# Splitting a scan of decays around an inverse, and spreading the loads of two chunks

## The chip, the cores and the metric

The kernel runs on one core of a Trainium2 chip. What is compared is the device time of one launch in microseconds (us), from runs of the same program on the same inputs. The core has five instruction streams that matter here. TensorE (PE in the profile) multiplies matrices, VectorE (DVE), ScalarE (ACT) and GpSimd (POOL) work elementwise, and SyncE (SP) gives out nearly all transfers (DMA). Each works through its own list in order, and waits for the others by semaphores.

## The reference

There are two parts, one behind the other. The first is a recurrence over 768 time steps, for 4 batches and 8 heads of width 40. Each head has a 40 x 40 state:

```
for t in range(S):
    y[:, :, t] = einsum('bhd,bhde->bhe', rt, state)
    Sa = einsum('bhde,bhe->bhd', state, at)
    state_decay = state * wt[:, :, None, :] - einsum('bhd,bhe->bhde', Sa, bt)
    state = state_decay + einsum('bhd,bhe->bhde', vt, kt)
```

The second part takes y as 3072 tokens of 320 numbers: `h = x @ w_in`, `g = h * cos(h)`, `out = g @ w_out`, with 2048 hidden numbers per token. The weights w_in and w_out arrive in 64-bit floating point, all other inputs in 32-bit.

## The kernel before, in words

**Chunks.** Time is cut into 24 chunks of 32 steps. The four batches lie on the four blocks of 32 partitions, so one tile holds one chunk of all batches and heads. Within a chunk the recurrence becomes matrix products with a triangular inverse per head and batch. From chunk to chunk only the state goes on, in the tile qz.

**Preparing a chunk.** `p1` has four parts for two chunks at a time: `p1_w` (decays), `p1_a` (a times the decays, aT), `p1_b` (b over the decays, turned: bT) and `p1_n` (their products, nps, copied to nt). `over_w` takes 1/w on VectorE (L395, rw) and b times that on POOL (L396, bn). `p2` prepares k, v and r of one chunk (vT, rT, kT, gram). `main(c)` is the chain of a chunk, in five steps t, q, x, s, z: the state turned (sT), qps, x0ps, sps, and dps with the new state (L754 on VectorE, L755 on POOL) and the outputs yt. `tokens` stores yt to DRAM (xd, L775) and its `back` loads it again as the tokens' tile xT (L785, L787). The second part multiplies xT.

**The decays.** For chunks 0 to 3 the running products of w are taken on the turned tile (L374). For chunks 4 and up they are taken beforehand, for four chunks at once, in the tile ws of 128 x 32 x 40. `ws_fetch(q)` loads it from w (L161, 640 KB). `ws_scan(q)` multiplies it in place in two halves: five instructions upward (L170) and four downward (L175), all on VectorE. `ws_store(q)` writes it to DRAM as wd (L180, 640 KB). `load(c, "w")` of a chunk from 4 on reads wd. `scanned(q)` is the scan, with the store two steps later and the next fetch twelve steps later. There is one tile ws, so a fetch needs the store before it to be done. In the part before the main loop `scanned(1)` comes right after chunks 0 to 3 are prepared, ahead of the inverse.

**The inverse.** `by_blocks(0)` holds its steps for chunks 0 to 3: a transpose of nt (L486, u), 15 pairs of instructions (L520, L525), and two transposes (L534, L502: the tile rt). `pair_first` and `pair_second` fill in the lower half with products on TensorE (below), and VectorE adds it (L567) before step s of that chunk may use rt.

**The weights.** They are rounded from 64-bit to 32-bit words in 20 units. Each unit is fetched by SP (L237, words), opened on VectorE (L245, L246), completed by `mantissa` (L255, with ScalarE at L258), and multiplied together (L261 on VectorE, L264 on POOL). Fetching a unit takes a buffer that an earlier one has to give back: unit 10 takes that of unit 7, unit 14 that of unit 11.

**What sets the order.** All is written out by hand. The order of the calls is the order in each engine's list. `step(work, of_inv, of_w)` makes a step, then counts down the works that wait in a list, then gives out some steps of the inverse and of the weights. `later(n, work)` puts a work into that list, to be given out after n more steps. Works that fall to the same step go in the order in which they were put in. Most of them are loads, and SP's list is in order: a DMA that waits for its data or its buffer holds up all behind it.

**Loads.** `load(c, names)` gives out four DMAs of 40 KB, one per batch, in pieces of 160 bytes (L152). Chunks 0 and 1, and 4 and up, take turns in two tiles for each of w, a and b (nat_w, nat_a, nat_b). Chunks 2 and 3 lie for the time being in parts of the weights' tiles (that of b in w_out_sb). Chunks 4 and 5 are loaded by a list at the end of the part before the main loop (L1028); chunks 6 and up by `p1` itself.

**The main loop.** For each chunk c a list `segs` names the steps of the chunk's chain, those of the next chunks' preparation, and places M for pieces of the second part. In chunks 1 and 2, the steps F and S are `pair_first` and `pair_second`. In chunk 3, `pw4`, `pa4`, `pb4` and `pn4` prepare chunks 4 and 5. `busy` and `kept_busy` are matmuls on a tile of zeros that keep TensorE at work.

Of the kernel before, what the change touches and what calls it, by code (L numbers as in the profile page):

```python
# [20 lines left out]
def kernel(  # L21
# [124 lines left out]
    def load(c, names, via=nc.sync, parts=range(B)):  # L146
        for n in names:
            for i in parts:
                at_c = src[n][i, :, c * C : (c + 1) * C, :]
                if n == "w" and c >= 4:  # L150
                    at_c = wd[c // 4][i, :, c % 4]
                via.dma_start(nat[n, c][blk[i], :, :D], at_c.rearrange("h t d -> t h d"))  # L152
# [6 lines left out]
    def ws_fetch(q, via=nc.sync):  # L159
        n = 4 * C * D  # L160
        via.dma_start(  # L161
            ws.rearrange("p t d -> p (t d)"),
            bass.AP(w.tensor, w.offset + q * n, [[S * D, B * H], [C * D, 4], [1, C * D]]),
        )

    def ws_scan(q):
        n = 1
        while n < C:
            to = ws[:, 2 * n - 1 :: 2 * n]
            nc.vector.tensor_tensor(to, to, ws[:, n - 1 :: 2 * n], ALU.mult)  # L170
            n *= 2
        n = C // 4
        while n:
            to = ws[:, 3 * n - 1 :: 2 * n]
            nc.vector.tensor_tensor(to, to, ws[:, 2 * n - 1 : C - 1 : 2 * n], ALU.mult)  # L175
            n //= 2

    def ws_store(q):
        wd[q] = dram.tile([B, H, 4, C, D], F32, tag="wd", name="wd")
        nc.sync.dma_start(wd[q].rearrange("b h c t d -> (b h c) (t d)"), ws.rearrange("p t d -> p (t d)"))  # L180
# [5 lines left out]
    load(1, "a", nc.scalar)  # L186
    for n, c in (("w", 2), ("w", 3), ("a", 2), ("a", 3), ("b", 2)):
        load(c, n)
    ws_fetch(1)
    load(3, "b")  # L190

# [149 lines left out]
    def later(steps, work):  # L343
        waiting.append([steps, work])

    def step(work, of_inv=0, of_w=0, small=False):


        before = list(waiting)
        work()  # L350
        G["small"] = small and G["kind"]
        for w in before:
            w[0] -= 1
            if w[0] == 0:
                waiting.remove(w)
                w[1]()
        for steps, n in ((inv_steps, of_inv), (w_steps, of_w)):
            for _ in range(min(n, len(steps))):
                steps.pop(0)()
# [186 lines left out]
    def pair_first(c, i, moe=True):  # L546
        ps = pair_space(c, moe, ps_h, "h")
        nt = G["noff"].rearrange("p c e j t -> p (c e j) t")
        half = pair_half(c, i)
        for n in range(H):  # L550
            for g in range(B):
                mm(
                    ps[blk[g], HB * n : HB * (n + 1)], nt[blk[g], H * i + n, :],
                    G["rn"][blk[g], H * i + n, :], n == 0,
                )
        nc.scalar.copy(half[:, :, :HB], ps[:, : H * HB].rearrange("p (n u) -> p n u", u=HB))
        if c + i == 3:
            nc.gpsimd.memset(padding(bn_b[6]), 0.0)
# [347 lines left out]
    def scanned(q):  # L906

        ws_scan(q)
        later(2, lambda: ws_store(q))
        if q + 1 < NCH // 4:  # L910
            later(12, lambda: ws_fetch(q + 1))
# [17 lines left out]
    with tc.manual_schedule():  # L929
# [63 lines left out]
        w_work[1][0]()  # L993
        for seg in (other[1], *first[2:], *other[2:]):
            step(seg)
        scanned(1)
        p2_in(0)
        p2_kn(0)
        inv_space()
# [17 lines left out]
        step(g1)  # L1017
        busy(3)
        N_PAD = {0: 0, 19: 60}
        step(lambda: pair_first(0, 0, False), 0, 2)  # L1020
        for m in range(3, 5):
            w_work[m][0]()
        step(lambda: pair_second(0, 0, False), 0, 2)
        step(s0, 0, 4)
        busy(6)
        step(z0, 0, 2)
        busy(4)
        for n, c, name in ((1, 4, "a"), (3, 4, "w"), (5, 5, "w"), (6, 5, "a"), (7, 5, "b"), (9, 4, "b")):  # L1028
            later(n, lambda c=c, name=name: load(c, name))

        done = 0
# [17 lines left out]
        for c in range(NCH):  # L1049
            t, q, x, s, z = main(c)  # L1050
            v, k, g = p2(c + 1) if c + 1 < NCH else [lambda: None] * 3
            q0 = c - c % 4 + 4
            fill, pn, pn4 = (1, 4), None, None
            if c == 0:
                segs = []
            elif c == 1:
                segs, fill = [t, F1, v, q, k, S1, x, g, s, z], (1, 4)
            elif c == 2:
                segs, fill = [t, F2, v, q, S2, k, M, x, M, F3, g, M, s, S3, M, z, M, M], (0, 2)
            elif c == 3:  # L1060
                pw4, pa4, pb4, pn4 = p1(4)
                pw, pa, pb, pn = p1(6)
                segs = [
                    t, pw4, M, q, pa4, M, x, lambda: scanned(2), M, s, pw, M, pb4, pa, M, pn4, M, z, M,
                    pb, v, pn, k, M, g,
                ]
                fill = (2, 3)
            elif c == 4:
                pw, pa, *p8 = p1(8)
                firsts = [lambda n=n: pair_first(4, n) for n in range(4)]  # L1070
                seconds = [lambda n=n: pair_second(4, n) for n in range(4)]
                F4, F5, F6, F7 = firsts
                S4, S5, S6, S7 = seconds
                segs = [
                    t, v, M, q, M, k, x, M, F4, M, S4, F5, M, s, F6, M, pw, F7, M, z, M, g, M, pa, S5, lambda: scanned(3),
                ]
                fill = (2, 0)
            elif c == 5:
                pw, pa = p1(10)[:2]
                pb, pn = p8  # L1080
                segs = [t, M, pb, q, M, pn, k, M, x, M, s, S6, M, z, M, S7, M, pw, v, M, g, pa, M]
            elif c % 4 == 0 and q0 < NCH:
                pb, pn = p1(q0)[2:]
                segs = [t, v, M, q, M, k, x, M, g, M, s, pb, M, z, M, pn, M, M]
                if q0 + 4 < NCH:
                    segs.insert(-1, lambda: scanned(c // 4 + 2))
            elif c % 4 == 1 and q0 < NCH:
                pw, pa = p1(q0 + 2)[:2]
                segs = [t, M, pw, q, M, x, k, M, s, v, M, z, M, pa, M, g, M, M]
            elif c % 4 == 2 and q0 < NCH:  # L1090
                pb, pn = p1(q0 + 2)[2:]
                segs = [t, M, pb, q, M, pn, v, M, x, M, s, k, M, g, M, z, M, M]
            elif c % 4 == 3 and q0 + 4 < NCH:
                pw, pa = p1(q0 + 4)[:2]
                segs = [t, M, pw, q, M, x, k, M, s, v, M, z, M, pa, M, g, M, M]
            else:
                segs = [t, v, M, q, M, x, k, M, g, M, s, M, M, z, M, M]
            n = len(segs)

            goal = 8 * (c + 1) - (18 if c < 19 else 20)  # L1100
            empty, places = 0, segs.count(M)
            if c > 3:
                empty = max(0, min(places - (goal - done), 2 if c < 8 else places))
                goal = max(goal, done + places - empty)
            place = 0
            if c == 19:
                shifted(N_PAD[c])
            for i, seg in enumerate(segs):
                kept_busy(FILL.get((c, i), 0))
                while seg is s and ("rt", c) not in G:  # L1110
                    if allowed(c):
                        piece(4, 0)
                    else:
                        inv_steps.pop(0)()
                while seg is pn4 and w_steps:
                    w_steps.pop(0)()
                if seg is not M:
                    G["kind"] = "q" if seg is q and c > 3 else "other"
                    step(seg, *((0, 0) if c < 3 and seg in (*firsts, *seconds) else fill), small=seg in (q, x, g, s, z, pn, pn4, *firsts, *seconds))
                    if seg not in (*firsts, *seconds) and (c < 2 or c == 2 and not done):  # L1120
                        busy({s: 6, q: 5, v: 4, k: 4, z: 4}.get(seg, 3))
                else:
                    place += 1
                    if place * empty // places > (place - 1) * empty // places:
                        continue
                    if allowed(c) and (c != 4 or done < 23):
                        piece(*fill)
                while i == n - 1 and c > 3 and done < goal and c != 4 and allowed(c):
                    piece(*fill)
                if seg is pn and (c == 3 or c > 4 and c % 4 == 2):  # L1130
                    inv_steps.extend(by_blocks(q0) if c == 3 else inverse(q0))
# [36 lines left out]
```

## Time and profile before

| | us |
|---|---|
| median of 3 runs | 807.01 |
| lowest and highest | 802.86, 811.95 |
| the profiled execution | 806.77 |
| its span, first to last instruction | 805.0 |
| TensorE busy in it | 752.7 |
| VectorE busy | 487.0 |
| ScalarE busy | 387.8 |
| POOL busy | 201.1 |

The durations below come from the profiled execution. Its own time is 1.77 us longer than its span. The granted clock of TensorE is 0.973 of full speed on average. In the page's slices a digit is the busy share in tenths. Timelines give the start, the busy time, the engine, the line, the operation, the tile written and the tiles read, how often, and in brackets the idle time before it with what ended it. "SPq" is SP giving out a DMA: its time is that of issuing, not of the transfer.

### The profile page before, as it was taken

What the parts mean: (1) busy time and instruction counts of PE and PEld (TensorE: products, weight loads), DVE (VectorE), ACT (ScalarE), POOL (GpSimd) and SP (SyncE); (2) the same over time, 40 slices, a digit from 0 to 9 for tenths busy, and PEclk for the clock granted to TensorE, in tenths of its full rate; (3) what the DMA queues carried; (4) which work ended last, traced back from release to release, by engine and by line L of the source; (5) the groups of instructions that cost most, each with busy time, mean ns of one, the idle gap of its engine ahead of it and who ended that gap; (6) DMA issues with size and microseconds to landing.
All of it is one profiled execution on the core that took longest, in us unless ns stands there. A gap on an engine that the chain in (4) does not pass through costs nothing.

```text
span 805.0 us, 39600 instructions
## 1 busy us (share of the span) xinstructions
PE 752.7 (94%) x17812; PEld 575.5 (71%) x17812; DVE 487.0 (60%) x1025; ACT 387.8 (48%) x723; POOL 201.1 (25%) x354
## 2 busy tenths in 40 slices
PE   5777698999999999999999999999999999999997
PEld 4544376777777777777777777777787777777775
DVE  8779658864734796553895644994346873333231
ACT  1337467555425435545435635535645445354352
POOL 5316535320322220330330230332131122201000
PEclk9688799999999999999999999999999999999999
DMA  8666552354253324334214314223220222101000
GB/s 114 176 162 149 143 145 74 57 121 65 59 125 58 66 38 71 72 92 67 60 40 69 94 36 72 53 45 69 46 46 21 46 46 49 24 17 34 19 17 16
DMA packets 183303, 55.78 MB, mean 69 GB/s; under 512 B 157152, under 2 KB 178656, under 8 KB 183136
## 3 DMA queue, kind: packets, MB, share of 16 engines
q1 hardware_dynamic: 177440, 52.11, 30.1%
q8 instruction: 140, 2.29, 1.2%
q10 hardware_dynamic: 5440, 0.82, 0.7%
q0 software_dynamic: 256, 0.33, 0.2%
q14 instruction: 27, 0.22, 0.1%
HBM read 42.07 MB, written 11.14 MB: 66 GB/s over the span
## 4 chain that ended last, share of the span: by engine, by line
PE 66%; DVE 18%; ACT 4%; issue 4%; DMA 3%; SPq 3%; POOL 1%; DVEq 0%; ACTq 0%; POOLq 0%
PE ph L101 23%; PE po L101 19%; PE x0ps L101 3%; PE dps L101 3%; SPq L152 3%; DVE inv_tmp L494 3%; DVE rw L395 3%; PE vT L330 3%; PE gram L101 2%; DVE inv L498 2%; PE sps L101 2%; PE nps L101 2%; PE qps L101 2%; PE sT L654 1%; DMA nat_a<-in_a_dram 1%
## 5 line engine op out<-in xcount | busy, mean ns | idle before, releaser
L101 PE MATMUL po<-w_out_sb,gT 128*128 128x320 f32 x768 | 223.1, 439 | 0.0
L101 PE MATMUL ph<-xT,w_in_sb 128*128 128x256 f32 x768 | 187.0, 388 | 0.3 <-issue 0.3
L101 PEld LDWEIGHTS po<-w_out_sb,gT 128*128 128x128 f32 x768 | 140.2, 190 | 54.2 <-issue 1.7
L101 PEld LDWEIGHTS ph<-xT,w_in_sb 128*128 128x128 f32 x768 | 140.1, 191 | 30.4 <-issue 12.5
L829 ACT ACTIVATE turns<-ph,rnd 128x512 f32<-128x512 f32 x96 | 64.1, 686 | 157.7 <-PE ph L101 157.3
L831 DVE SCALAR_TENSOR_TENSOR turns<-turns,ph 128x512 f32<-128x512 f32 x96 | 64.1, 685 | 111.7 <-ACT turns L829 111.4
L839 DVE TENSOR_TENSOR gT<-ph,turns 128x512 f32<-128x512 f32 x96 | 65.8, 687 | 39.1 <-ACT turns L836 39.1
L755 POOL TENSOR_TENSOR qz<-qz,wc 128x160 f32<-128x160 f32 x92 | 42.4, 480 | 167.1 <-DVE qz L754 166.5
L836 ACT ACTIVATE turns<-turns,half_pi 128x512 f32<-128x512 f32 x96 | 69.4, 723 | 3.1
L835 ACT ACTIVATE turns<-turns 128x512 f32<-128x512 f32 x96 | 60.2, 627 | 18.9 <-DVE turns L831 18.9
L101 PE MATMUL ph<-xT,w_in_tail 64*128 64x256 f32 (+1 forms) x512 | 54.9, 393 | 1.3 <-issue 1.3
L498 DVE TENSOR_TENSOR inv<-inv,inv_tmp 128x31 f32<-128x31 f32 (+15 forms) x124 | 51.2, 413 | 4.3
L754 DVE TENSOR_TENSOR qz<-dps,qz 128x160 f32<-128x160 f32 x92 | 29.2, 318 | 36.2 <-PE dps L101 36.0
L586 POOL COPY vp<-nat_v 128x320 f32<-128x320 f32 x24 | 11.9, 494 | 156.3 <-DMA nat_v<-in_v_dram 135.8
L494 DVE TENSOR_TENSOR inv_tmp<-u,inv 128x31 f32<-128x31 f32 (+15 forms) x124 | 48.6, 392 | 2.3
L395 DVE RECIPROCAL rw<-nat_w 128x320 f32<-128x320 f32 x20 | 42.9, 2144 | 0.1
L658 ACT COPY s<-sT 128x512 f32<-128x512 f32 x46 | 24.5, 585 | 35.1 <-PE sT L654 35.1
L101 PEld LDWEIGHTS ph<-xT,w_in_tail 64*128 64x128 f32 (+1 forms) x512 | 32.5, 160 | 10.4 <-issue 6.8
L766 POOL TENSOR_TENSOR yt<-yt,wb 128x512 f32<-128x512 f32 x24 | 31.9, 1329 | 22.3 <-DVE yt L761 22.3
L718 DVE TENSOR_TENSOR sm<-sps,su 128x128 f32<-128x128 f32 x48 | 11.7, 286 | 32.1 <-ACT sm L713 29.3
L396 POOL TENSOR_TENSOR bn<-nat_b,rw 128x320 f32<-128x320 f32 x22 | 20.1, 914 | 43.6 <-DVE rw L395 37.2
L642 ACT COPY vvm<-gram 128x256 f32<-128x256 f32 x24 | 8.8, 369 | 43.6 <-DVE ag L637 43.2
(136 smaller groups left out, 1127.9 us busy)
## 6 DMA issues: line engine op xcount, KB each, us to landing
words<-in_moe_w_in_dram SPq DMA_DIRECT2D x8, 512.0 KB
xd<-yt SPq DMA_DIRECT2D x48, 80.0 KB
out_dram<-ot SPq DMA_DIRECT2D x24, 160.0 KB
nat_k<-in_k_dram SPq DMA_DIRECT2D x92, 40.0 KB
nat_v<-in_v_dram SPq DMA_DIRECT2D x92, 40.0 KB
nat_r<-in_r_dram SPq DMA_DIRECT2D x92, 40.0 KB
nat_a<-in_a_dram SPq DMA_DIRECT2D x84, 40.0 KB
ws<-in_w_dram SPq DMA_DIRECT2D x5, 640.0 KB
```

The lines of the kernel that those rows point to most:

```text
L101: nc.tensor.matmul(o, lhsT=lhsT, rhs=rhs, start=start, stop=stop, skip_group_check=True)
L395: nc.vector.reciprocal(rw, wn)
L494: nc.vector.tensor_tensor(tmp, u[:, j : j + 1, :j].to_broadcast([P, C - j, j]), x[:, j:, j : j + 1].to_broadcast([P, C - j, j]), ALU.mult,)
L498: nc.vector.tensor_tensor(x[:, j:, :j], x[:, j:, :j], tmp, ALU.subtract)
L754: nc.vector.tensor_tensor(z, pick(dp, 0, (2 * N72 + C, 2), (N72, 2), (1, D)), z, ALU.add)
L755: nc.gpsimd.tensor_tensor(z, z, wc.rearrange("p (f m b) -> p f m b", f=2, m=2)[:, :, :, bb] .unsqueeze(3).to_broadcast([P, 2, 2, D]), ALU. ...
L766: nc.gpsimd.tensor_tensor(yt.rearrange("p j b t -> p (j b) t"), yt.rearrange("p j b t -> p (j b) t"), wx, ALU.mult)
L829: nc.scalar.activation(n, u, ACTF.Identity, bias=rnd, scale=1.0)
L831: nc.vector.scalar_tensor_tensor(n, n, -ROUND, u, ALU.add, ALU.subtract)
L835: nc.scalar.activation(n, n, ACTF.Abs)
L836: nc.scalar.activation(n, n, ACTF.Sin, bias=half_pi, scale=-2.0 * math.pi)
L839: nc.vector.tensor_tensor(gT[:, 2 * e : 2 * e + 2].rearrange("p f t -> p (f t)"), us[e], ns[e], ALU.mult)
```

## The change

The scan is cut in two functions, `ws_up` and `ws_down`. Before the main loop only `ws_up` stands where `scanned(1)` stood. `ws_down` comes behind the inverse of chunks 0 to 3 and the steps k1 and g1, ahead of the first `pair_first`. The store of the result is then put three steps, and the next fetch of ws 17 steps, behind step s of chunk 0. Later scans (`scanned(2)` and on) stay in one piece.

The load of b of chunk 3 moves ahead of the first fetch of ws.

Of the six loads of chunks 4 and 5 in the list at L1028 only the two of a stay there, that of chunk 5 one step earlier. The w of both and the b of chunk 4 are given out in the course of chunk 2, and the b of chunk 5 in that of chunk 3.

```diff
     def ws_scan(q):
+        ws_up()
+        ws_down()
+
+    def ws_up():
         n = 1
         while n < C:
             to = ws[:, 2 * n - 1 :: 2 * n]
             nc.vector.tensor_tensor(to, to, ws[:, n - 1 :: 2 * n], ALU.mult)
             n *= 2
+
+    def ws_down():
         n = C // 4
...
     for n, c in (("w", 2), ("w", 3), ("a", 2), ("a", 3), ("b", 2)):
         load(c, n)
+    load(3, "b")
     ws_fetch(1)
-    load(3, "b")
...
-        scanned(1)
+        ws_up()
         p2_in(0)
...
         N_PAD = {0: 0, 19: 60}
+        ws_down()
         step(lambda: pair_first(0, 0, False), 0, 2)
         for m in range(3, 5):
             w_work[m][0]()
         step(lambda: pair_second(0, 0, False), 0, 2)
         step(s0, 0, 4)
+        later(3, lambda: ws_store(1))
+        later(17, lambda: ws_fetch(2))
         busy(6)
         step(z0, 0, 2)
         busy(4)
-        for n, c, name in ((1, 4, "a"), (3, 4, "w"), (5, 5, "w"), (6, 5, "a"), (7, 5, "b"), (9, 4, "b")):
+        for n, c, name in ((1, 4, "a"), (5, 5, "a")):
             later(n, lambda c=c, name=name: load(c, name))
...
             elif c == 2:
+                for n, m, name in ((2, 4, "w"), (11, 5, "w"), (15, 4, "b")):
+                    later(n, lambda m=m, name=name: load(m, name))
                 segs, fill = [t, F2, v, q, S2, k, M, x, M, F3, g, M, s, S3, M, z, M, M], (0, 2)
...
+                for n, m, name in ((1, 5, "b"),):
+                    later(n, lambda m=m, name=name: load(m, name))
                 fill = (2, 3)
```

## The prediction

> **What bounds the kernel now.** I read the page first, for where TensorE is the bound and where it is not.
>
> ```profile
> span 805.0 us, 39600 instructions
> PE 752.7 (94%) x17812; PEld 575.5 (71%) x17812; DVE 487.0 (60%) x1025; ACT 387.8 (48%) x723; POOL 201.1 (25%) x354
> ...
> PE   5777698999999999999999999999999999999997
> DVE  8779658864734796553895644994346873333231
> ```
>
> A slice is 20.1 us. From slice 6 (about 120 us) TensorE is at nines to the end, with its instructions in a fixed order; before it, it is not, and that time is paid in full. So a gain or loss in the first 120 us moves the end by about as much, and a later one counts only if TensorE has to wait. All that the change moves lies in or next to the first 150 us.
>
> Next the waits of the window 62 to 130 us, the chain of 84 to 104 us, and the timeline around the longest wait.
>
> ```profile
> DVE mant L245 <- DMA words<-in_moe_w_in_dram: 5.2, 1, 5.2
> ```
> ```profile
> 86.40 5.80 DMA words<-in_moe_w_in_dram
> ```
> ```profile
> 73.79 1.92 SPq L152 DMA_DIRECT2D nat_w<-wd  x4
> ...
> 79.06 3.28 SPq L152 DMA_DIRECT2D nat_a<-in_a_dram  x4
> ...
> 82.38 1.93 SPq L152 DMA_DIRECT2D nat_r<-in_r_dram  x4
> ...
> 84.41 1.89 SPq L152 DMA_DIRECT2D nat_b<-in_b_dram  x4
> ...
> 86.40 0.39 SPq L237 DMA_DIRECT2D words<-in_moe_w_in_dram  x1
> ...
> 86.88 1.88 SPq L152 DMA_DIRECT2D nat_b<-in_b_dram  x4
> ...
> 92.30 0.43 DVE L245 TENSOR_SCALAR mant<-words 128x512 int32<-128x512 int32 x1 [5.22 <-DMA words<-in_moe_w_in_dram]
> ```
>
> VectorE waits 5.22 us for unit 10 of the weights (units 0 to 19; L245 opens each, so this is its eleventh). Its buffer was free at 79.0, when the last reader of unit 7 ended (L255, 78.35 + 0.68), but its DMA went out at 86.40 only: SP's queue is in order and gave out loads without a gap from 69.9. Behind that wait stand the four qz of chunk 1 (L754, 93.58), so chunk 2 too. By one-microsecond windows nothing at all runs from 89 to 92.
>
> ```profile
> 90.00:91.00 1.00, 0.00 (x0) 0.00 (x0) 0.00 (x0) 0.00 (x0) 0.00 (x0) 1.00 0.82 184
> ```
>
> Last the timeline of 17 to 62 us, for the scan and the inverse.
>
> ```profile
> 18.99 0.68 SPq L161 DMA_DIRECT2D ws<-in_w_dram  x1
> 19.71 2.06 SPq L152 DMA_DIRECT2D w_out_sb<-in_b_dram  x4
> ...
> 25.13 0.95 POOL L396 TENSOR_TENSOR bn<-w_out_sb,rw 128x320 f32<-128x320 f32 x1 [3.19 <-DVE ws L170]
> ...
> 26.47 2.81 DVE L175 TENSOR_TENSOR ws<-ws 128x40 f32<-128x40 f32 x4
> ...
> 31.99 1.25 DVE L486 STREAM_TRANSPOSE u<-nt 128x1024 f32<-128x1024 f32 x1 [2.71 <-ACT nt L459]
> ...
> 49.53 0.28 DVE L567 TENSOR_TENSOR rt<-rt,below 128x128 f32<-128x128 f32 x1
> ```
>
> The inverse starts at 31.99 because b of chunk 3 lands late (24.97 by the chain, whatever releaser POOL's line names), and from there bn, bT, nps and nt follow one another. The scan is not what it waits for: VectorE is idle for 2.71 us behind it.
>
> **What the Trainium skill says.** "DMA: Bandwidth & Descriptors", Queues, rings and completion order: each DMA engine consumes descriptors in ring order. The trace agrees: unit 10 goes out at 86.40, but the packets of 86 to 88 us are small ones of b (796 of 812), and the large ones follow from 88. Same page, Specifications: 512 B are the least for line rate; of the packets of 84 to 93 us, 3028 of 3349 are smaller, and they move 83 GB/s in 84 to 86 us at a DMA share of 0.55. "GPSIMD Engine Reference", Key points: GpSimd shares its SBUF interfaces with VectorE and contends with instructions of two SBUF inputs. It agrees: the four L175 take 2.81 us at 26.47 with POOL at work, 1.81 us at 151.73 with POOL nearly idle.
>
> **The change part by part.**
>
> *b of chunk 3 ahead of the fetch of ws.* Its issue starts 0.7 us earlier, and the 640 KB of ws (their large packets fill 20.5 to 22.7 us) no longer lie before it in the rings. Its packets ran at 22.7 to 24.0; without ws they end at about 22.3. Then bn waits for rw and aT of chunk 3 (23.0 to 23.6) in place of 25.13: 1.5 to 2.0 us earlier, and bT, nps, nt and L486 with it; I take 1.7. The bounds: 0.7 if only the issue counts, 2.1 if rw alone does.
>
> *The scan's first half.* ws goes out at 21.1 and lands by about 25.5 (before: out 18.99, landed by 23.66, so 4.7 us or less). Its five L170 took 2.88 us: done by 28.4, two microseconds before L486 at 30.3. Free under that wait; if ws lands later than 27.4, each microsecond costs one.
>
> *The scan's second half behind the inverse.* It stands on VectorE behind L643 (ends 48.27) and ahead of the weights' L245 and L246 and of L567. Queued behind it: L567, whose rt TensorE needs for sps (49.87), so the chain of chunk 0. POOL has nothing from 39.2 to 52.9, so I take 1.81 us; the bounds are 1.8 and 2.8. With the inverse 1.7 earlier, L567 is at 49.53 - 1.7 + 1.8 = 49.6: **+0.1 us**, bounds -0.3 and +2.1.
>
> *Store of the decays (640 KB) and fetch of the next ws.* They leave SP at 34.7 (1.34 us) and 55.16 (1.55 us). The store now stands on SP ahead of chunk 0's xd (62.31), while SP waits for yt: 0.4 to 1.5 us to issue, up to 0.6 of it beyond that wait, and its bytes, at some 210 GB/s 3 us, lie ahead of xd in the rings. xT, behind which SP stands until xd has landed (66.13 before), comes 0 to 2.4 us later; I take 1.2. Chunk 0's xT itself is needed at 106.94 only. The fetch of ws goes behind unit 14, in chunk 2.
>
> *Loads taken out of chunk 1.* w of 4 (63.05, 2.04 us): nothing, as SP waited for xd to 66.13 anyway. w of 5 (73.79, 1.92 us) and b of 5 (84.41, 1.89 us) stand ahead of unit 10: 3.8 us. b of 4 (86.88) stands behind it, but shares the rings: 600 small packets in 89 to 90 us. a of 5 stays, a step earlier. So unit 10 goes out at 86.40 - 3.8 + 1.2 = 83.8 and, with the small packets gone, lands 4 us later (5.8 before; 4.0 is the median from issue to landing of POOL's loads of b): 87.8. VectorE reaches it at 87.07 + 0.1 = 87.2. L245 moves from 92.30 to about 88: **-4.3 us**, bounds -5.1 (no wait left) and -2.7 (xT late by 2.4, landing as slow).
>
> *Loads put into chunks 2 and 3.* SP goes out continuously from 101.5 to 116.3. w of 4 (2.0 us) comes between xd and xT of chunk 1, where SP waits 1.6 us anyway: 0.4 us on xT, nat_k and unit 14. The fetch of ws (0.6 to 1.5 us) comes ahead of unit 15, out at 112.54 and used at 119.43; its 640 KB take about 3 us of the rings, less than the 6.9 us there. w of 5 (2.0) and b of 4 (2.0) fall around the idle stretch 116.3 to 121.5, b of 5 into 136.6 to 141.1. They are needed at 133.3 (wT), 141.1 and 146.5 (bn): covered by 9 us or more; without that cover bn would hold up POOL's qz. What can tell is unit 14: out at 106.19, used at 111.30, with VectorE now 4.3 us earlier and SP's added 0.4, and a ring in front that w of 4 fills. I book **+0.8 us**, between 0 and 3.
>
> The sum: +0.1 is already inside the -4.3, so -4.3 + 0.8 = **-3.5 us** on the profiled execution's 806.77 us (its span of 805.0 and 1.8 around it), 803.3. That execution is 0.2 us below the median of 807.01 (802.86 to 811.95), so no correction is needed.
>
> **The rivals.** *No change:* the wait is off by the 2.7 us of the low bound and is lost again at unit 14 (3 us): 807. For it: VectorE has only 3.8 us between the end of unit 14's issue (107.5) and its use. Against: VectorE waits 1.39 us for turns (114.04) right after, which swallows part of it.
>
> *Slower, the stall moves on:* w of 4 and the 640 KB of ws in chunk 2 hit units 14 and 15 as the old loads hit unit 10. Its price is that stall again, 5.2 us, and the second half at its uncovered 2.8 us less the 0.7 from b: 806.8 - 4.3 + 5.2 + 2.1 = 809.8. It decides from the point where unit 15 lands more than 6.9 us after its issue, or unit 14 more than 4. Against: DMA was half idle there (0.44 in 100 to 110 us, 0.33 in 120 to 130).
>
> *More than reckoned:* TensorE also has gaps of 1.2 to 3.6 us in 63 to 93 us that it waits for nothing shown ("issue"). "Runtime: NRT & Kernel Launch", Instruction fetch mechanics, says that instructions come in 16 KiB blocks by a DMA queue of their own; the page's 140 packets of 2.29 MB are of that size, and one ran in the crowded 89 to 90 us. If less traffic shortens them, VectorE's 1.48 us for x at 77.38 and the whole 5.2 go, with 1.5 of the later stages' gaps: 806.8 - 8.2 = 798.6. That these gaps are fetches is not shown.
>
> **How the numbers follow.** Forecast (801.5 to 805.5) 0.47; no change (805.5 to 808) 0.19; slower 0.14; more 0.20. A measurement of this kernel can tell about 1%, 8 us. Faster by over 1% (under 799) takes most of the last case and a little of the forecast's scatter: 0.20; slower by over 1% (over 815) needs the moved stall to repeat at a second unit, or late decays to hold TensorE at wT: 0.09; the rest 0.71. The range 797.5 to 810 leaves out 1 in 10 on either side.
>
> **What would show it.** Right: L486 near 30.3; L175 of about 1.8 us behind L643; L567 within a microsecond of 49.5; unit 10 out by 85 and VectorE's wait for words under 1.5 us; L754 of chunk 1 near 89.5. Wrong: a new wait of L245 for words between 100 and 120 us, wT waiting for nat_w, POOL's bn waiting for nat_b, or SP standing long before xT at 66 to 70.

## The result and the profile after

The changed kernel takes 803.99 us in the median of 22 runs (799.99 to 809.21), the kernel before 806.85 us (22 runs, 802.44 to 811.95). The ratio is 0.9973, with a 95% interval of 0.9953 to 0.9992: 2.9 us less were measured and 3.5 were forecast. Run again beside other experiments it gave 0.9979 (0.9957 to 1.0000). Ratios here and below leave out the few executions that were over 1.5% above the fastest of their kernel, and they are not the quotients of the medians.

The profiled execution of the changed kernel is one of its longer ones: 806.41 us, against 806.77 of the one before. So the two spans hardly differ, and what the medians show has to be looked for earlier. From the changed page, its span, TensorE's busy time and its slices:

```profile
span 804.7 us, 39599 instructions
PE 753.0 (94%) x17812; PEld 577.0 (72%) x17812; DVE 485.7 (60%) x1025; ACT 387.1 (48%) x723; POOL 199.8 (25%) x354
...
PE   4678798999999999999999999999999999999997
```

The work is the same, and TensorE is as full as before from slice 6 on. The difference lies ahead of it. VectorE's waits for the weights, 62 to 130 us, in the changed kernel:

```profile
DVE mant L251 <- DMA words<-in_moe_w_out_dram: 1.0, 1, 1.0
DVE mant L251 <- DMA words<-in_moe_w_in_dram: 0.2, 1, 0.2
```

The wait of 5.2 us for unit 10 has come down to 0.2, and a new one of 1.0 us stands before unit 14. (The change adds six lines, so L245 is L251 now, L754 is L760, L486 is L492, L567 is L573.) SP's queue and VectorE around it:

```profile
63.24 0.43 SPq L186 DMA_DIRECT2D wd<-ws  x1
63.95 2.16 SPq L781 DMA_DIRECT2D xd<-yt  x2
70.18 0.40 SPq L791 DMA_DIRECT2D xT<-xd  x1
...
82.67 1.94 SPq L152 DMA_DIRECT2D nat_r<-in_r_dram  x4
84.71 7.12 SPq L243 DMA_DIRECT2D words<-in_moe_w_in_dram  x6
...
88.95 0.43 DVE L251 TENSOR_SCALAR mant<-words 128x512 int32<-128x512 int32 x1 [0.23 <-DMA words<-in_moe_w_in_dram]
```

Unit 10 is the first of the six DMAs at 84.71. It landed 4.14 us later by the chain of waits, and VectorE opened it at 88.95 in place of 92.30. But SP stood before xT until 70.18 (66.13 before), behind the store of ws at 63.24. The start, in the changed kernel's timeline:

```profile
21.46 0.69 SPq L161 DMA_DIRECT2D ws<-in_w_dram  x1
...
23.36 0.86 POOL L402 TENSOR_TENSOR bn<-w_out_sb,rw 128x320 f32<-128x320 f32 x1 [1.27 <-DMA w_out_sb<-in_b_dram]
...
26.30 2.22 DVE L174 TENSOR_TENSOR ws<-ws 128x640 f32<-128x640 f32 x5 [2.74 <-DMA ws<-in_w_dram]
...
30.45 1.38 PE L101 MATMUL nps<-aT,bT 40*32 40x32 f32 x108 [3.92 <-issue]
...
32.92 1.25 DVE L492 STREAM_TRANSPOSE u<-nt 128x1024 f32<-128x1024 f32 x1 [4.40 <-ACT nt L465]
...
49.02 1.81 DVE L181 TENSOR_TENSOR ws<-ws 128x40 f32<-128x40 f32 x4
...
52.09 0.28 DVE L573 TENSOR_TENSOR rt<-rt,below 128x128 f32<-128x128 f32 x1
```

The bn is 1.8 us earlier than before, as reckoned. Then TensorE stops for 3.92 us in the middle of nps (1.16 before, at the same product), and the inverse starts 0.9 us later than before and not 1.7 earlier. L573 is 2.6 us late. So the change lost about two microseconds in the start and won more than that back at unit 10. TensorE's clock is not what made this gain: from 92 to 100 us it was 0.66 and 0.50 before and 1.00 in this profile, but in the second profile of the changed kernel it was 0.54 and 0.61 from 88 to 96 us, and the gain in chunk 1 is as large there.

One measure serves for all that follows: the start of POOL's outputs yt (the line after qz) of one chunk. Differences to the kernel before, in us, in the two profiles of the changed kernel:

| chunk | 0 | 1 | 2 | 3 | 4 | 10 | 18 | 23 |
|---|---|---|---|---|---|---|---|---|
| before, at | 60.55 | 97.46 | 130.31 | 165.83 | 206.40 | 391.00 | 623.55 | 750.66 |
| changed | +1.7 | -3.4 | -2.7 | -2.3 | -1.8 | -1.5 | -1.3 | -0.1 |
| changed, again | +0.5 | -4.3 | -3.9 | -3.4 | -1.1 | -1.9 | -1.4 | -1.0 |

The gain is made in chunk 1, and part of it goes again between chunks 1 and 4. In the first profile 1.2 us more goes between chunks 18 and 19, where TensorE stops from 638.12 to 639.25 us; the second profile has no stop there.

### The profile page after: what moved, and what is told of

Read it like the earlier page. It is cut to its first block, busy times and chain, and to the rows that moved or that the text cites. A ratio compares the mean times of both kernels' runs of the same rounds, so it can differ in the third digit from the quotient of the medians.

```text
span 804.7 us, 39599 instructions
## 1 busy us (share of the span) xinstructions
PE 753.0 (94%) x17812; PEld 577.0 (72%) x17812; DVE 485.7 (60%) x1025; ACT 387.1 (48%) x723; POOL 199.8 (25%) x354
## 4 chain that ended last, share of the span: by engine, by line
PE 64%; DVE 15%; ACT 5%; DMA 5%; issue 4%; POOL 2%; SPq 2%; DVEq 0%; ACTq 0%; POOLq 0%
PE ph L101 22%; PE po L101 20%; PE x0ps L101 3%; PE dps L101 3%; DVE rw L401 3%; PE gram L101 3%; PE vT L336 2%; PE nps L101 2%; DVE inv_tmp L500 2%; DVE inv L504 2%; PE sps L101 2%; PE qps L101 2%; SPq L152 1%; PE bT L336 1%; DVE turns L837 1%
## 5 line engine op out<-in xcount | busy, mean ns | idle before, releaser
L760 DVE TENSOR_TENSOR qz<-dps,qz 128x160 f32<-128x160 f32 x92 | 28.8, 313 | 36.5 <-PE dps L101 36.4
```

What stands on the lines that cost most here:

```text
L760: nc.vector.tensor_tensor(z, pick(dp, 0, (2 * N72 + C, 2), (N72, 2), (1, D)), z, ALU.add)
```

## The experiments

What each run gave, one line each. "Gap" is TensorE's time without a shown cause inside the nps of chunks 2 and 3, and "inverse" the start of the transpose u. "xT" is when SP gives out xT of chunk 0 (all times in us), "unit 10" is VectorE's wait for it, and "yt 1" is the start of chunk 1's yt. These come from the one profile of each. The ratio to the kernel before, with its 95% interval, comes from 12 to 22 runs.

| run | gap | inverse | xT | unit 10 | yt 1 | ratio |
|---|---|---|---|---|---|---|
| before | 1.16 | 31.99 | 66.13 | 5.22 | 97.46 | 1 |
| changed | 3.92 | 32.92 | 70.18 | 0.23 | 94.11 | 0.9973 (0.9953-0.9992) |
| changed, again | 2.87 | 31.99 | 68.74 | 0.71 | 93.15 | 0.9979 (0.9957-1.0000) |
| loads alone | - | 31.74 | 66.94 | - | 93.08 | 0.9943 (0.9925-0.9962) |
| b ahead alone | 2.81 | 31.94 | 68.84 | 2.59 | 96.09 | 1.0003 (0.9977-1.0029) |
| loads in old places | 2.94 | 31.26 | 68.11 | 7.55 | 98.49 | 1.0067 (1.0046-1.0088) |
| scan whole | 2.01 | 30.55 | 68.39 | 1.96 | 92.85 | 0.9966 (0.9949-0.9983) |
| store later | 2.93 | 31.25 | 66.48 | 1.08 | 93.75 | 0.9969 (0.9947-0.9991) |
| scan and store early | 2.94 | 31.42 | 67.85 | - | 92.91 | 0.9953 (0.9933-0.9973) |
| scan in chunk 2 | 1.78 | 30.39 | 64.43 | - | 90.48 | 0.9963 (0.9945-0.9981) |
| loads alone, later | - | 30.66 | 65.22 | - | 91.10 | 0.9928 (0.9903-0.9952) |
| the same again | 0.92 | 31.86 | 65.94 | - | 91.83 | 0.9950 (0.9930-0.9970) |
| changed, loads later | 2.81 | 31.22 | 68.31 | 1.60 | 93.17 | 0.9971 (0.9950-0.9991) |
| scan and store early, loads later | 3.51 | 32.36 | 66.28 | - | 92.13 | 0.9958 (0.9939-0.9977) |

A dash is no gap, or no wait, of over a quarter of a microsecond.

**The loads alone.** The kernel before, with only this:

```diff
-        for n, c, name in ((1, 4, "a"), (3, 4, "w"), (5, 5, "w"), (6, 5, "a"), (7, 5, "b"), (9, 4, "b")):
+        for n, c, name in ((1, 4, "a"), (5, 5, "a")):
...
+                for n, m, name in ((2, 4, "w"), (11, 5, "w"), (15, 4, "b")):
+                    later(n, lambda m=m, name=name: load(m, name))
...
+                for n, m, name in ((1, 5, "b"),):
+                    later(n, lambda m=m, name=name: load(m, name))
```

> The kernel before with only the loads of chunks 4 and 5 put where the change puts them; scan, store, fetch of ws and b of chunk 3 as before. Theory (the gain is unit 10 no longer behind loads on SP): unit 10 goes out near 82.6 us, VectorE's wait for words falls from 5.2 to under 1, the first L754 of chunk 1 comes at 88.5 to 90 (93.58 before), and the time is 3 to 5 us below the kernel before, as good as the whole change or better. Rival (the gain comes from b and the split scan): no more than 0.5 us below the kernel before.

The ratio is 0.9943, 4.5 us less in the medians: all of the change's gain, and in the medians 1.6 us more. In its timeline:

```profile
81.59 9.64 SPq L237 DMA_DIRECT2D words<-in_moe_w_in_dram  x6
...
89.50 0.32 DVE L754 TENSOR_TENSOR qz<-dps,qz 128x160 f32<-128x160 f32 x1
```

Unit 10 goes out 4.8 us earlier than before, without any wait for it left, and the first qz comes at 89.50 (93.58 before). The rival, that the gain comes from b and the scan, falls.

**The loads in their old places**, all else as changed.

```diff
-        for n, c, name in ((1, 4, "a"), (5, 5, "a")):
+        for n, c, name in ((1, 4, "a"), (3, 4, "w"), (5, 5, "w"), (6, 5, "a"), (7, 5, "b"), (9, 4, "b")):
...
-                for n, m, name in ((2, 4, "w"), (11, 5, "w"), (15, 4, "b")):
-                    later(n, lambda m=m, name=name: load(m, name))
...
-                for n, m, name in ((1, 5, "b"),):
-                    later(n, lambda m=m, name=name: load(m, name))
```

> The changed kernel with the six loads of chunks 4 and 5 back where they were; split scan, later store and fetch, and b ahead kept. Theory: the wait for words is back (4 us or more), with w of chunk 4 now also behind the store of ws on SP; L760 of chunk 1 at 94 to 97, time 1 to 3 us above the kernel before. Rival (the split pays by itself): 1 us or more below the kernel before.

1.0067, 4.5 us above: without the moved loads the rest of the change costs time, more than expected. Its timeline:

```profile
66.22 1.79 SPq L152 DMA_DIRECT2D nat_w<-wd  x4
68.11 0.39 SPq L791 DMA_DIRECT2D xT<-xd  x1
...
85.80 3.20 SPq L152 DMA_DIRECT2D nat_b<-in_b_dram  x4
89.11 0.39 SPq L243 DMA_DIRECT2D words<-in_moe_w_in_dram  x1
...
93.81 0.43 DVE L251 TENSOR_SCALAR mant<-words 128x512 int32<-128x512 int32 x1 [7.55 <-DMA words<-in_moe_w_in_dram]
```

The wait for unit 10 has grown to 7.55 us, as unit 10 goes out only at 89.11. Chunk 1's yt is just 1.0 us late, but chunk 2's is 4.6 late. TensorE stood for 6.5 us before chunk 1's sT, and by windows of four microseconds its granted clock was 0.59, 0.50 and 0.63 from 92 to 104 us, where the kernel before was back at 0.99 from 100.

**b ahead alone.** The kernel before, with one line moved:

```diff
+    load(3, "b")
     ws_fetch(1)
-    load(3, "b")
```

> The kernel before with only b of chunk 3 ahead of the fetch of ws, the scan whole in its old place. Theory (TensorE's gap behind the 20th product of nps takes back what b gains): bn near 23.4 (25.13 before), a gap of about 4 us in nps (1.16 before), L486 at 32.5 to 33 (31.99 before), time 0 to 1 us above the kernel before. Rival (as predicted: an earlier b is an earlier inverse): L486 at 30.3 to 31.5, time 0.5 to 1.7 below.

1.0003, with a median 1.2 us below the kernel before: no difference is shown. The bn came at 23.36, as in the changed kernel, and then

```profile
29.55 1.29 PE L101 MATMUL nps<-aT,bT 40*32 40x32 f32 x108 [2.81 <-issue]
...
31.94 1.25 DVE L486 STREAM_TRANSPOSE u<-nt 128x1024 f32<-128x1024 f32 x1 [2.16 <-ACT nt L459]
```

nps went on at 29.55, where it did before (29.51). The 1.8 us at bn became gap: 2.81 us of it, where about 4 were expected, and L486 at 31.94 in place of 32.5 to 33.

The DMA packets in the traces show what TensorE waited for. Packets of 16 KB on a queue of their own (q8, of the kind "instruction") bring its instructions; the last section gives the grounds. The first of them after the start belongs to this place in nps. It landed at 28.07 us in the kernel before and at 28.21 here. TensorE was done with the matmuls ahead of the place at 28.36 before and at 26.74 here, and went on 1.44 and 1.34 us after the landing. So the gap lasts until a packet is there that does not come earlier when b does.

**The scan whole, in its old place,** all else as changed:

```diff
         ws_up()
+        ws_down()
         p2_in(0)
...
-        ws_down()
         step(lambda: pair_first(0, 0, False), 0, 2)
```

> The changed kernel with the second half of the scan back in front of the inverse, right behind the first; all else as changed. Theory (in this order the inverse waits for TensorE's nps, and not for the scan): ws lands near 26.3, both halves end near 30.5, the inverse starts at 32.9 as in the changed kernel, L573 comes at about 50.3 in place of 52.09, and the time is 0.5 to 1.8 us below the changed kernel. Rival (the split is what keeps the inverse from waiting): the inverse starts 1 us or more later, time equal to the changed kernel or above it.

L573 came at 48.15, 3.9 us earlier than with the split, and the inverse did not wait for the scan: it waited 0.23 us for nt at 30.55. Of the 3.9 us, 2.4 are the earlier inverse of this profile (30.55 against 32.92) and 1.6 the scan: from the start of the inverse to L573 it took 17.6 us, and 19.2 in both profiles of the changed kernel. Yet the median is 803.96 us, the changed kernel's. Chunk 1's yt is only 1.3 us earlier, since now VectorE waits 1.96 us for unit 10: SP was still held up before xT, to 68.39. The reading that fits is that the split costs slack of VectorE in the start, as long as SP is the later one. So the expectation held for L573 in its direction (about 50.3 was expected), but not for the time.

**The store of ws later:**

```diff
-        later(3, lambda: ws_store(1))
+        later(8, lambda: ws_store(1))
```

> The changed kernel with the store of ws five steps later, behind xd and xT of chunk 0, and nothing else. Theory (the store's 640 KB lie in front of xd, and SP stands before xT until that has landed): xT goes out near 67 in place of 70.2, unit 10 of the weights near 82 in place of 84.7, the wait for words is gone, but VectorE is no earlier, so L760 of chunk 1 at 90 and the time within 0.7 us of the changed kernel. Rival (SP's order sets chunk 1): L760 of chunk 1 earlier by 2 us or more, time 2 us below the changed kernel.

0.9969, within a microsecond of the changed kernel. xT went out at 66.48 in place of 70.18. From the issue of xd to that of xT it took 3.73 us, as in the kernel before (3.82), and 6.23 in the changed kernel, so the store does lie in front of it, as the theory said. Unit 10 did not gain by it:

```profile
82.22 0.45 SPq L186 DMA_DIRECT2D wd<-ws  x1
82.78 7.78 SPq L243 DMA_DIRECT2D words<-in_moe_w_in_dram  x6
```

The 640 KB of the store now came right before unit 10, and the wait was 1.08 us, where none was expected. The edit had moved the cost from xT to unit 10; it says nothing on a store that is out of both ways.

**Scan and store in the old places,** b ahead and the later second fetch kept:

```diff
         ws_up()
+        ws_down()
+        later(2, lambda: ws_store(1))
         p2_in(0)
...
-        ws_down()
         step(lambda: pair_first(0, 0, False), 0, 2)
...
-        later(3, lambda: ws_store(1))
```

> The changed kernel with the scan whole in its old place and the store two steps behind it, as in the kernel before; b ahead, the later fetch and the spread loads kept. So it is the loads alone with b ahead and a later second fetch. Theory (with the scan whole, L573 is 2 to 4 us earlier, and only SP's late xT kept that from showing): xT at 65 to 67, unit 10 out by 81, no wait for words at unit 10, L760 of chunk 1 at 87 to 89, time 4 to 5.5 us below the kernel before. Rival (the store's place does not matter): L760 of chunk 1 as with the scan whole and the later store, time 3 us below.

0.9953, 4.3 us below in the medians, with no wait for unit 10. The time is as the theory had it, and chunk 1 as the rival had it: its yt comes at 92.91, and at 92.85 with the scan whole and the store in its changed place. xT at 67.85 and unit 10 at 82.78 are later than expected too. The two ratios (0.9953 and 0.9966) differ by less than their intervals.

**The scan in chunk 2.** ws is fetched behind the inverse, and scanned around step x of chunk 2, where the changed kernel's VectorE waited 3.25 us:

```diff
     load(3, "b")
-    ws_fetch(1)
...
-        ws_up()
         p2_in(0)
...
-        ws_down()
+        ws_fetch(1)
         step(lambda: pair_first(0, 0, False), 0, 2)
...
-        later(3, lambda: ws_store(1))
-        later(17, lambda: ws_fetch(2))
...
-                for n, m, name in ((2, 4, "w"), (11, 5, "w"), (15, 4, "b")):
+                for n, m, name in ((11, 4, "b"), (13, 4, "w"), (15, 5, "w")):
                     later(n, lambda m=m, name=name: load(m, name))
+                later(9, lambda: ws_store(1))
+                later(17, lambda: ws_fetch(2))
+                x = (lambda run: lambda: (ws_up(), run(), ws_down()))(x)
```

> The changed kernel with the whole scan taken out of the part before the loop: ws is fetched ahead of the first pair_first, both halves of the scan stand around step x of chunk 2 (where VectorE waited 3.25 us for x), the store follows in chunk 2, and w of 4 and 5 are loaded after it. Theory (what eats the gain of an earlier b is the 640 KB of ws in front of TensorE's gap in nps, and the store of ws holds up xT): the gap in nps falls to about 1 us, the inverse starts near 29.5, xT goes out near 65, the first L760 of chunk 1 comes at 86 to 89, and the time is 4 to 7 us below the kernel before. Rival (the gap in nps has nothing to do with ws): gap of 2 us or more, L760 of chunk 1 at 89 to 90, time 2 to 4 us below.

The start behaved as the theory had it, though the gap shrank less:

```profile
28.06 1.24 PE L101 MATMUL nps<-aT,bT 40*32 40x32 f32 x108 [1.78 <-issue]
```

The gap is 1.78 us, less than in all nine profiles with b ahead and ws behind it (2.01 to 3.92), and more than in the four with b behind ws (1.16 at most). That ws has a part in it is not shown by this: the packet of instructions landed at 26.88 us, inside the range of those nine (26.56 to 28.97), and two units of 512 KB each still follow b. Chunk 1's yt is the earliest of all, 7.0 us before the kernel before. The ratio is 0.9963 all the same, 3.8 us below in the medians: of the 7.0 us, 3.3 were left at chunk 4 (203.11 against 206.40) and 2.9 at chunk 23. Loads of w that go out only behind the store, and a second fetch in the same chunk, come with this edit; which of them takes the gain was not tried.

**The loads alone, later.** In the kernel with the loads alone:

```diff
-                for n, m, name in ((2, 4, "w"), (11, 5, "w"), (15, 4, "b")):
+                for n, m, name in ((11, 4, "w"), (15, 5, "w"), (16, 4, "b")):
```

> The loads alone, with w of 4 nine steps, w of 5 four steps and b of 4 one step later, so that no load of w or b stands ahead of unit 14 of the weights. Theory (w of 4 ahead of unit 14 costs part of the gain): VectorE's wait of 2.07 us for unit 14 falls under 1, POOL's outputs of chunk 2 start 0.5 to 1.5 us earlier than with the loads alone (127.6), and the time is 0.5 to 1.5 us below it. Rival (that wait is covered by what follows): same time within 0.5 us.

800.18 us in the median of 12 runs, 0.9928, 2.2 us below the loads alone in the medians (0.5 to 1.5 were expected). VectorE had waited 2.07 us for unit 14 with the loads alone; that wait is gone, and chunk 2's yt starts at 123.32 (127.61). Its SP queue shows that w of 4 now stands behind units 14 and 15:

```profile
99.32 2.47 SPq L237 DMA_DIRECT2D words<-in_moe_w_out_dram  x3
...
107.33 0.87 SPq L237 DMA_DIRECT2D words<-in_moe_w_out_dram  x2
...
109.78 1.91 SPq L152 DMA_DIRECT2D nat_w<-wd  x4
```

Once more, beside the changed kernel on one chip:

> The loads alone, put later, once more, beside the changed kernel on one chip. Theory: 5 to 7 us below the kernel before and 2 to 4 below the changed kernel; clock of TensorE at 1.0 from 90 to 140 us. Rival (the first time was a good draw): 3.5 to 5 below, as the loads alone in their first places.

802.89 us and 0.9950 (805.65 for the kernel before there), 2.8 below the kernel before and 1.2 below the changed kernel beside it. VectorE waited 0.58 us for unit 14. TensorE's clock was 1.00 from 90 to 140 us, as expected. So the first time was a good draw: the two ratios give 4 to 6 us, and the expectation of 5 to 7 was too high. Against the loads alone in their first places (0.9943) nothing can be told.

**The changed kernel again:**

> The changed kernel once more, for a second profile and beside the three others. Theory (what the first profile showed in the start is the rule, and the lower clock at 124 to 128 us follows from TensorE's gap of 2.1 us ahead of it): a gap of 2 to 4 us in nps, L492 at 30.5 to 33, xT out at 68 to 70.5, VectorE's wait for unit 10 under 2 us, and wherever TensorE stands still for over 2 us near 120 to 125, a clock under 0.8 behind it; time 2 to 4 us below the kernel before. Rival (the first profile was a bad draw): gap under 2, xT before 68.

Gap, xT and the wait for unit 10 repeat within what was expected; the time is 1.6 us below the kernel before in the medians, a little less than the 2 expected. The clock did not fall at 124 to 128 us this time, with a gap of 1.85 us ahead of it.

**The changed kernel with the loads later** (the same edit as above):

> The changed kernel with w of 4 nine steps, w of 5 four and b of 4 one step later, as in the best of the runs with the loads alone. Theory (w of 4 ahead of unit 14 costs 1 to 2 us wherever it stands, and the rest of the change costs 1 to 3): no wait at unit 14, POOL's outputs of chunk 2 near 126, time 3.5 to 5 us below the kernel before, and 1 to 3 above the loads alone put later. Rival (the rest of the change costs nothing): within 0.7 us of the loads alone put later.

0.9971. Unit 14's wait is gone, but chunk 2's yt is at 128.99, no better than in the changed kernel. TensorE's gap ahead of chunk 1's sT was 2.82 us, and its clock 0.56 and 0.59 from 92 to 100 us. In the medians it is 0.4 us below the loads alone put later, and by the ratios 1.7 above, so between the theory and its rival nothing can be told. The later loads took away VectorE's wait for unit 14 in this setting, and took it away or shortened it in the other; a gain in time from them is shown in neither.

**Scan and store early, with the loads later** (two of the edits above together):

> The changed kernel with scan whole and store in the old places, b ahead and the later fetch kept, and the loads put later. Theory (b ahead gains at most 1 us, since TensorE's gap takes the rest back, and the later fetch costs nothing): within 1 us of the loads alone put later. Rival (b ahead and the later fetch cost by themselves): 1 to 3 us above it.

802.84 us, the loads alone put later at 802.89 beside it: b ahead and the later fetch neither gain nor cost what could be measured. Its profile has a gap of 3.51 us in nps, and VectorE still waits 1.97 us for unit 14, although no load of w or b stands ahead of it. Other loads and the second fetch of ws went out around it; which of them delays it was not tried.

**A faster version.** The loads alone, in either place, come out below the changed kernel in all three measurements (0.9943, 0.9928, 0.9950 against 0.9973 and 0.9979), by 1.2 us in the medians of the one batch that had both. There the means of the 22 runs on each side differ by 1.9 us (804.15 and 802.21), and resampling these runs gives a 95% interval of 0.6 to 3.3 for the means, but -0.8 to 3.6 for the medians. So it is very likely faster than the changed kernel, by one to three microseconds; which part of the change costs this was not separated.

## Why the prediction was right, step by step

*The loads taken out of chunk 1: right, and shown.* Unit 10 was to go out at 83.8, land 4 us later and take VectorE's wait away. It went out at 84.71 and landed 4.14 us later; the wait was 0.23. L251 came 3.35 us earlier, not 4.3. The two runs that separate the loads from the rest (0.9943 with them alone, 1.0067 without) show that this is the whole gain. That the landing fits is luck: the 4 us came from POOL's loads of b, 40 KB each, and unit 10 has 512 KB. Nor are the small packets shown to be what delayed it before. With b ahead alone the loads of chunks 4 and 5 stand where they did, and from the issue of unit 10 to L245 it took 4.24 us, as in the changed kernel, against 5.90 before. The low bound of -2.7 is also missummed: an xT late by 2.4 and a landing in 5.8 us put unit 10 at 90.8, which leaves -1.4.

*b ahead: the step failed at "and bT, nps, nt and L486 with it; I take 1.7".* The bn moved by the 1.77 us that was reckoned. The chain behind it did not. The prediction had TensorE's 1.16 us without a cause inside nps in view, and let it move along with the work. It was a wait for a packet of instructions, which landed at 28.07 us before and at 26.56 to 28.97 with b ahead, while TensorE came to that place 1.6 to 2.5 us earlier. With b ahead the gap was 2.0 to 3.9 us, and the start of the inverse lies between 30.55 and 32.92 in nine profiles (median 31.4), against 30.66 to 31.99 in the four without (median 31.8). What is left of the 1.7 is about 0.4 in the medians, less than the scatter.

*First half: right.* ws landed at 26.2 by VectorE's wait (25.5 predicted), the five instructions took 2.22 us, and ended over four microseconds before L492.

*Second half: its price right, its effect not.* The four took 1.81 us, exactly as taken from the profile. (POOL was not nearly idle at 151.73, as the prediction has it, but at work on small copies and memsets for half of that time; here it was idle, with the same 1.81.) L573 came 2.6 us late and not 0.1, as the inverse was not earlier. That it cost so little in the end was luck of the order: VectorE had slack against unit 10. With the scan whole L573 is 3.9 us earlier, and the time the same. In the end VectorE came to unit 10 at 88.72 in place of 87.2, and unit 10 landed at 88.85 in place of 87.8: two delays side by side, of which only the longer counts.

*The store: mis-sized.* xT was put at 1.2 us later, at most 2.4; it was 4.05 and 2.6 later in the two profiles. Part is yt's own delay (1.65 us in the first), the rest the 640 KB in front of xd: with the store out of that way xT went out at 66.48. So xT was 2.85 us later than reckoned in the first profile, but unit 10 only 0.91: from xT to unit 10 SP needed 14.53 us, where 20.27 less the 3.8 of the two loads, 16.5, were reckoned. These 0.91 are most of the 0.95 us that L251 missed; VectorE's own delay ran beside them.

*The loads put into chunks 2 and 3: about right.* +0.8 us was booked for unit 14, which VectorE waited 0.96 us for in the first profile and not at all over a quarter of a microsecond in the second. The cover of wT and bn held: neither waited for w or b of 4 and 5. But 1.6 to 3.2 us of the gain went between chunks 1 and 4, more than that.

*Where that went.* From chunk 1's yt to chunk 4's it took 108.9 us before, 108.9 and 109.7 with the loads alone put later, and 110.5 to 115.1 in the eleven other profiles, b ahead alone (111.0) among them, where no load of chunks 4 and 5 was moved. So not all of it can be the moved loads. In the first profile, 1.4 us is TensorE's clock. The groups of po behind chunk 2's dps in the changed kernel's timeline:

```profile
124.90 0.50 PE L101 MATMUL dps<-sm,bn 32*40 32x72 f32 x14 [2.13 <-issue]
125.33 5.97 PE L101 MATMUL po<-w_out_sb,gT 128*128 128x320 f32 x16
```

The stretch ahead of them and their own in the changed kernel, then the stretch with the same stop in its second profile. The second figure is TensorE's busy time, the third from the right the granted clock:

```profile
121.36:124.77 3.41, 1.42 (x118) 1.25 (x118) 1.89 (x3) 3.20 (x6) 1.00 (x1) 1.00 0.34 116
124.77:128.19 3.42, 3.29 (x20) 2.12 (x20) 2.71 (x10) 1.56 (x3) 2.30 (x5) 0.50 0.48 153
```
```profile
122.45:125.86 3.41, 1.96 (x20) 1.44 (x20) 2.61 (x9) 3.13 (x5) 1.11 (x3) 1.00 0.36 99
```

The end of the same dps in the timeline of the kernel before, which had a stop there too:

```profile
127.75 0.36 PE L101 MATMUL dps<-sm,bn 32*40 32x72 f32 x14 [1.27 <-issue]
```

The same 16 matmuls took 4.57 to 4.58 us in twelve of the fourteen profiles, and 5.97 and 6.26 us in the changed kernel and with the loads alone, both with a clock of 0.8 or less there. "TensorE: Matmul & The Clock Gate", Part 1, in the Trainium skill lets the clock fall after an idle window of some 3.4 us. On the length the traces agree: in all fourteen the clock is 1.00 or 0.50, and holds for a whole number of stretches of 3.41 us. That the window has to be idle throughout they contradict: the stop was 2.13 us, and TensorE was busy for 1.42 us of the stretch after which the clock fell. The stop of 1.85 us in the second profile, with 1.96 us busy in its stretch, left the clock at 1.00. In the second profile of the changed kernel it was not the clock: TensorE waited 0.6 us for xT, and had gaps of 1.5 and 0.7 us in gram and nps, between 155 and 180 us. Whether these are the price of the changed loads or chance can't be told from single profiles, and stays open.

*The rivals.* "The stall moves on" did not happen: the new wait at unit 14 was 1 us and not 5.2, and nothing waited for unit 15. "More than reckoned" rested on shorter gaps of TensorE in 63 to 93 us. In sum they did shorten, from 8.7 us to 5.0 and 4.3, and the time gained no more than was forecast: the longest, of 3.64 us, lay in VectorE's wait for unit 10, and behind it TensorE waited 2.02 us more for yt. The forecast's own case held, with an L573 that was 2.5 us worse than reckoned. That the sum came out so near is in part luck: at chunk 4 the two profiles have 1.8 and 1.1 us left of their gain, and the medians of the two measurements 2.9 and 1.6.

## What to carry to other kernels

A queue that is in order is read like an engine: what a load costs is told by what stands behind it, and here three loads with 30 us and more to spare stood before one that VectorE was about to wait for. An earlier input is worth only as much as the chain behind it lets through, and a gap without a shown cause in that chain is not work that moves along: it can grow by as much as the input is early. Here it was a wait for instructions, and these came no sooner with b ahead (28.21 us, against 28.07). And a wait that several engines share hides what each of them costs: with the wait gone, each has to be priced again.

## What the runs showed of the hardware

TensorE's gaps without a cause stand at fixed places of its list. Counted in its order of the 17812 matmuls, those of over a microsecond in the first 100 us come before the matmuls 212, 466, 721, 848, 976, 1103, 1358, 1486 and 1741 (counted from 0) in one profile or another, and nowhere else. The differences are 127 or 128 or a sum of these. A matmul and its weight load are two instructions, so that is one block of 256, which is what the Trainium skill ("Runtime: NRT & Kernel Launch", Instruction fetch mechanics) gives for a 16 KiB block. From the page before:

```profile
q8 instruction: 140, 2.29, 1.2%
```

140 packets of 256 instructions are 35,840, while TensorE has 35,624 matmuls and weight loads. The times of these packets settle what the gaps are. The fourteen profiles have 141 gaps of over 0.6 us without a cause. Each ended 1.19 to 1.93 us after the landing of a q8 packet, and at one place it is the same packet in all profiles: the first before matmul 212, the fifth before 721, the eleventh before 1486. Where the packet had landed two microseconds or more before TensorE came, there was no gap. So these are waits for instructions.

The packet before matmul 212 itself took 1.20 us before and 0.99 in the changed kernel. What differs is when it started, 26.87 and 27.98 us, and when TensorE was done with the matmuls ahead of it, 28.36 and 26.52: of the 2.8 us by which the gap grew, 1.8 are TensorE's earlier arrival and 0.9 the later landing. The DMA engines were 88 to 100% busy from 24 to 29 us in the changed kernel. That the full rings delay the start of the packet fits this, and was not tried by itself: before, they were as busy (0.89 from 24 to 27 us) ahead of a packet that started 1.1 us earlier. Beyond 260 us one gap of over 0.6 us is left in all fourteen profiles, that of 1.13 us in the changed kernel, with the engines at a share of 0.01.

The three profiles in which the clock did not fall again between 84 us and the end of the matmuls are the shortest (spans of 797.0 to 798.2 us; the others 800.2 to 811.2). In all, a stretch of 3.41 us at full clock was followed by a fall only where TensorE was busy for less than 67% of it; stretches with 44 to 66% went either way. Where a stop of two microseconds lies in these stretches differs from run to run, so whether the clock falls looks to be in part chance.

The runs of one kernel spread by half a per cent to 2%, and the granted clock goes with it: over the 75 runs of the kernel before in the last batch, its mean lay between 0.961 and 0.980, with a correlation of -0.69 to the time, and some 5 us per hundredth (-0.53 and -0.49 in the two batches before). Which of the two makes the other is not shown. A difference of 0.3% needed 20 runs and more on either side.
